# Converting w_out in pieces of 384 columns with lo parts on VectorE, in a fused attention and squared-ReLU FFN kernel

## The chip, the cores and the metric

The kernel runs on one core of one Trainium2 chip. The metric is device time in microseconds of one execution, the median of several runs. In this text PE is TensorE, DVE VectorE, ACT ScalarE, POOL GpSimd and SP SyncE, as in the profile.

## The reference

Attention over 8 batches x 12 heads of 448 x 64, with normed q and k, gives x of 3584 tokens x 768. Then comes a feed-forward layer:

```python
def _moe_ref(x, w_in, w_out, s, b):
    h = x @ w_in                  # 3584 x 768 @ 768 x 2048
    r = np.maximum(h, 0.0)
    g = s * (r * r) + b
    return (g @ w_out).astype(np.float32)   # 3584 x 2048 @ 2048 x 768
```

w_in and w_out arrive as 64-bit floats; all else is 32-bit.

## The kernel before

Matmuls take operands rounded to a shorter 32-bit form (fp32r), so every operand is split into a hi part and a lo part (what the rounding left out), and a product is three matmuls: hi x hi, lo x hi, hi x lo.

There are two stages. In the first (lines 206 to 640) attention runs batch by batch, and beside it the first product, `ffn_in` (line 170), of the batch before. A *block* of it is 128 of the 2048 hidden columns for one batch of 448 tokens: 18 matmuls into a PSUM bank. `rectify` (189) has ACT take the ReLU out of the bank into a tile `r`, after which the bank is free, and `keep_r` (200) stores it to a DRAM buffer `r_d`.

The second stage (643 to 733) begins when attention is over and the last batch still has its 16 blocks of `ffn_in` to do. Beside these blocks, written out by hand in a fixed order for all engines but SP (`manual_schedule`, line 701; SP's order and everything behind that block are set by the framework's scheduler), two things are made ready for the second product:

- w_out (2048 x 768) in 48 *pieces* of 128 rows x 256 columns. `load_double` (115) is a generator: each `next` issues a step. SP loads the piece of 64-bit words (`w64o`, line 121). DVE puts the 32-bit float `wao` together from the two halves of each word in four instructions (124, 127, 129, 132), of which the last needs a square of the high half made by ACT (`wmo`, 125). Later ACT rounds it to the hi part `woh` (135) and POOL makes the lo part `wol` (136). The hi and lo parts are written over w_in's, quarter by quarter (`tag=wh{i}`, `wl{i}`): a quarter of w_in is four blocks' worth, so a piece that is put together at block m gets its hi and lo parts at block m + 4.
- The first three tiles of g, 128 tokens each. `squares` (652) is a generator as well: SP loads r for all 2048 columns (1 MB, line 659), ACT squares (665) and DVE scales (666); at the next step ACT rounds to `gh` (670) and DVE makes `gl` (671).

The loop over m (706 to 729) has 20 rounds: `ffn_in` for 16 of them (the work of round m on the other engines is also called block m's), three new pieces in each, and from round 4 on the hi and lo parts of three older ones. The tiles' loads are issued ahead of the loop (`chain(todo, first)`), their squares in rounds 7, 9, 11, and gh and gl in rounds 8, 10, 12. Buffers: 5 for `w64o`, 16 for `wao`, 3 for `wmo`, 2 for the tiles of r.

Behind it `ffn_out` (674) does the second product: first for tiles 0 to 2 together, quarter by quarter of w_out, then for the 25 others one by one. A tile is 96 matmuls, in two PSUM banks (`po`). Six banks for the first three tiles come from the list of free ones, whose order is that of the blocks that last used them: tile 0 gets the banks of blocks 8 and 9, tile 1 those of 10 and 11, tile 2 those of 12 and 13. So tile 2's first matmul waits for the ReLU of block 12.

Of the kernel before, what the change touches and what calls it, by code (L numbers as in the profile page):

```python
# [9 lines left out]
F32 = mybir.dt.float32  # L10
F32R = mybir.dt.float32r
I32 = mybir.dt.int32
AF = mybir.ActivationFunctionType
ALU = mybir.AluOpType
# [23 lines left out]
def attention_then_relu2_ffn(  # L38
# [30 lines left out]
    V, S, G, T = nc.vector, nc.scalar, nc.gpsimd, nc.tensor  # L69

    NPAIR, P, _, SEQ = kq.shape
# [12 lines left out]
    NFC = DF // P  # L84
    NKC = 4
    HALF = DM // 2
    NS = 4
    FS = DF // NS
    WI = 512
    WO = 256  # L90
    W = 8
    NSLOT = W * NPAIR

# [16 lines left out]
    def psum(name):  # L110

        bank = free.pop(0)
        return ps.tile([P, 512], F32, tag=bank, name=name), bank

    def load_double(room, dst_hi, dst_lo, src):

        w, a, m = room  # L120
        nc.sync.dma_start(w.rearrange("p n t -> p (n t)"), src)  # L121
        yield
        low, high = w[:, :, 0], w[:, :, 1]
        V.tensor_scalar(a, high, 3, 0x3FFFFFF8, ALU.logical_shift_left, ALU.bitwise_and)  # L124
        S.activation(m, high.bitcast(F32), AF.Square)  # L125
        yield
        V.scalar_tensor_tensor(a, high, -0x40000000, a, ALU.bitwise_and, ALU.bitwise_or)  # L127
        yield
        V.scalar_tensor_tensor(a, low, 29, a, ALU.logical_shift_right, ALU.bitwise_or)  # L129
        yield  # L130
        af = a.bitcast(F32)
        V.scalar_tensor_tensor(af, m.bitcast(F32), LEAST * LEAST, af, ALU.is_ge, ALU.mult)  # L132
        for _ in range(GAP):
            yield
        S.copy(dst_hi, af)  # L135
        G.tensor_tensor(dst_lo, af, dst_hi.bitcast(F32), ALU.subtract)  # L136
        yield

    w_in32 = w_in.bitcast(I32)
# [3 lines left out]
    def parts_of_w_in():  # L143

        for i in range(NS):
            whi[i] = wpool.tile([P, NCC, FS], F32R, tag=f"wh{i}", name=f"wih{i}")
            wlo[i] = wpool.tile([P, NCC, FS], F32R, tag=f"wl{i}", name=f"wil{i}")
            for c0 in range(0, FS, WI):
                for cc in range(NCC):
                    f0 = 2 * (i * FS + c0)  # L150
                    src = w_in32[cc * P : (cc + 1) * P, f0 : f0 + 2 * WI]
                    yield whi[i][:, cc, c0 : c0 + WI], wlo[i][:, cc, c0 : c0 + WI], src

    def parts_of_w_out():
        n = NFC // NS
        for i in range(NS):
            ohi[i] = wpool.tile([P, n, DM], F32R, tag=f"wh{i}", name=f"woh{i}")
            olo[i] = wpool.tile([P, n, DM], F32R, tag=f"wl{i}", name=f"wol{i}")
            for f in range(n):
                r0 = (i * n + f) * P  # L160
                for c0 in range(0, DM, WO):
                    c = slice(c0, c0 + WO)
                    src = w_out32[r0 : r0 + P, 2 * c0 : 2 * (c0 + WO)]
                    yield ohi[i][:, f, c], olo[i][:, f, c], src
# [24 lines left out]
    def rectify():  # L189

        while later:
            ph, bank, b, fc = later.pop(0)
            r = xp.tile([P, SEQ], F32, tag="r", bufs=2, name=f"r{b}_{fc}")
            S.activation(r, ph[:, :SEQ], AF.Relu)
            free.append(bank)
            kept.append((b, fc, r))
# [3 lines left out]
    def keep_r():  # L200

        while kept:
            b, fc, r = kept.pop(0)
            nc.sync.dma_start(r_d[b][fc], r)

    with tc.tile_pool(name="apool", bufs=1) as ap:
# [300 lines left out]
        def pieces():  # L507
            for i, (hi, lo, src) in enumerate(parts_of_w_in()):
                w = ap.tile([P, WI, 2], I32, tag="w64", name=f"w64i{i}")
                a = ap.tile([P, WI], I32, tag="wa", bufs=2, name=f"wai{i}")  # L510
                yield load_double((w, a, hi), hi, lo, src)

        def convert():

# [77 lines left out]
        with tc.manual_schedule(engines=ORDERED):  # L592
            begun = []
            for s_ in range(FIRST, NSLOT + START + 1):
# [17 lines left out]
                for f, a in jobs[s_]:  # L612
                    if f is next:
                        continue
                    g = f(*a)
# [18 lines left out]
                b, m = divmod(s_ + 1 - START, W * NP)  # L634
# [8 lines left out]
    with tc.tile_pool(name="opool", bufs=2) as op:  # L643

        def pieces():
            for i, part in enumerate(parts_of_w_out()):
                w = op.tile([P, WO, 2], I32, tag="w64", bufs=5, name=f"w64o{i}")
                a = op.tile([P, WO], I32, tag="wa", bufs=16, name=f"wao{i}")
                m = op.tile([P, WO], F32, tag="wm", bufs=3, name=f"wmo{i}")
                yield load_double((w, a, m), *part)  # L650

        def squares(t):
            r = op.tile([P, NFC, P], F32, tag="r2", bufs=2, name=f"r2_{t}")
            t0 = t * P
            while t0 < (t + 1) * P:
                b, off = divmod(t0, SEQ)
                n = min((t + 1) * P - t0, SEQ - off)
                o = t0 - t * P
                nc.sync.dma_start(  # L659
                    r[:, :, o : o + n],  # L660
                    r_d[b][:, :, off : off + n].rearrange("f p t -> p f t"),
                )
                t0 += n
            yield
            S.activation(r, r, AF.Square)
            V.tensor_scalar(r, r, sb_s, sb_b, ALU.mult, ALU.add)  # L666
            yield
            gh = op.tile([P, NFC, P], F32R, tag="gh", bufs=3, name=f"gh{t}")
            gl = op.tile([P, NFC, P], F32R, tag="gl", bufs=3, name=f"gl{t}")
            S.copy(gh, r)  # L670
            V.tensor_tensor(gl, r, gh.bitcast(F32), ALU.subtract)  # L671
            yield gh, gl

        def ffn_out(ts, gs):
            n = NFC // NS
            pos = [[psum(f"po{t}_{e}") for e in range(2)] for t in ts]
            for i in range(NS):
                for (gh, gl), po in zip(gs, pos):
                    for f in range(n):
                        fc = i * n + f  # L680
                        for m, (x, w) in enumerate(((gh, ohi[i]), (gh, olo[i]), (gl, ohi[i]))):
                            for e in range(2):
                                T.matmul(  # L683
                                    po[e][0][:, :HALF],
                                    x[:, fc, :],
                                    w[:, f, e * HALF : (e + 1) * HALF],
                                    start=fc == 0 and m == 0,
                                    stop=fc == NFC - 1 and m == 2,
                                )
            for t, po in zip(ts, pos):  # L690
                ot = op.tile([P, DM], F32, tag="ot", name=f"ot{t}")
                S.copy(ot[:, :HALF], po[0][0][:, :HALF])
                V.tensor_copy(ot[:, HALF:], po[1][0][:, :HALF])  # L693
                free.extend(bank for _, bank in po)
                nc.sync.dma_start(out[t * P : (t + 1) * P, :], ot)

        first = [squares(t) for t in range(3)]
        gs = []
        pieces = pieces()
        n = 3 * NFC // NS  # L700
        with tc.manual_schedule(engines=ORDERED - {ENGINE.SP}):
            waiting = []
            todo = list(islice(pieces, 3))
            for g in chain(todo, first):
                next(g)
            for m in range(NFC + NFC // NS):
                if m < NFC:
                    for _ in ffn_in(xs, *units[m]):
                        pass
                now, todo = todo, list(islice(pieces, 3))  # L710
                for g in todo:
                    next(g)
                old = waiting[:3] if m >= NFC // NS else []
                waiting = waiting[len(old) :]
                for step in range(4):
                    for g in now:
                        next(g)
                    if step == 1:
                        rectify()
                        keep_r()  # L720
                    if step == 2:
                        for g in old:
                            for _ in range(GAP):
                                next(g)
                waiting += now
                if m in (7, 9, 11):
                    next(first[(m - 7) // 2])
                if m in (8, 10, 12):
                    gs.append(next(first[(m - 8) // 2]))
        ffn_out([0, 1, 2], gs)  # L730
        for t in range(3, NT // P):
            *_, g = squares(t)
            ffn_out([t], [g])
# [44 lines left out]
```

## Time and profile before

| what | us |
|---|---|
| median of 3 runs | 1564.41 |
| lowest and highest of them | 1563.24, 1564.85 |
| the profiled execution's own time | 1564.78 |
| its span, first to last instruction | 1563.0 |
| PE busy with matmuls | 1466.8 |
| DVE busy | 904.3 |
| ACT busy | 816.0 |
| POOL busy | 735.6 |

The mean granted TensorE clock was 0.974 of full speed. In the profile an instruction is named by the line of the program, its engine, its operation and its tiles (out<-in, buffer numbers left out). A row of the timeline has the start and the length of a run of like instructions, and in brackets how long the engine stood idle ahead of it and what ended that. Where rows overlap, the time one instruction costs its engine is the distance to the next one's start. The releasers are worked out from semaphores: of several waits the last is named.

### The profile page before, as it was taken

How to read it: one execution, taken by the hardware profiler on the slowest of the kernel's cores; microseconds unless marked ns; L12 is line 12 of the kernel's file. 1: busy time of each engine (PE TensorE's matmuls, PEld its weight loads, DVE VectorE, ACT ScalarE, POOL GpSimd, SP SyncE). 2: the span in 40 equal slices, each digit the busy share in tenths (PEclk: the TensorE clock that was granted, in tenths of full speed). 3: DMA queues.
4: the chain of work that ended last, by engine and by line, in shares of the span. 5: the costliest groups of instructions: out<-in, count | busy, mean ns of one | idle time of the engine just before them, and what ended most of it. 6: DMA issues, size and time to landing. Idle time of an engine off the chain costs nothing. (4 is left out here: it accounts for less than half of the span.)

```text
span 1563.0 us, 21722 instructions
## 1 busy us (share of the span) xinstructions
PE 1466.8 (94%) x7380; PEld 1347.0 (86%) x7380; DVE 904.3 (58%) x1399; ACT 816.0 (52%) x1522; POOL 735.6 (47%) x611
## 2 busy tenths in 40 slices
PE   8775679999999999999999999997999999999998
PEld 7543468889989989989989989996899999999998
DVE  6986986776676776676676675269732222222210
ACT  4654646676676676766666666435442222222210
POOL 7586757667766767767767765215600000000000
PEclk9997789999999999999999999999999999999999
DMA  4465555666666666666666653276452322322300
GB/s 112 124 170 162 170 169 175 190 185 186 191 184 187 191 180 191 192 183 188 192 181 190 191 174 115 66 239 188 132 148 75 102 85 75 107 79 79 106 21 31
DMA packets 218751, 230.86 MB, mean 148 GB/s; under 512 B 72912, under 2 KB 193744, under 8 KB 218640
## 3 DMA queue, kind: packets, MB, share of 16 engines
q1 hardware_dynamic: 218640, 229.47, 49.4%
q8 instruction: 58, 0.95, 0.3%
q14 instruction: 53, 0.43, 0.1%
HBM read 177.21 MB, written 40.84 MB: 140 GB/s over the span
## 5 line engine op out<-in xcount | busy, mean ns | idle before, releaser
L177 PE MATMUL ph<-x,wih 128*128 128x448 f32 x1536 | 491.9, 367 | 0.0
L177 PEld LDWEIGHTS ph<-x,wih 128*128 128x128 f32 x1536 | 291.7, 190 | 23.5 <-issue 0.2
L415 ACT ACTIVATE st<-st 128x448 f32<-128x448 f32 x336 | 176.6, 526 | 239.4 <-PE st L399 236.3
L369 DVE TENSOR_REDUCE nmx<-sh 112x1 fp32r<-112x448 f32 x384 | 235.7, 618 | 112.4 <-PE sh L358 110.9
L177 PE MATMUL ph<-x,wil 128*128 128x448 f32 x768 | 284.6, 371 | 0.0
L683 PE MATMUL po<-woh,gh 128*128 128x384 f32 x896 | 230.1, 336 | 9.0 <-ACT gh L670 6.5
L683 PE MATMUL po<-wol,gh 128*128 128x384 f32 x896 | 229.9, 336 | 3.4 <-POOL wol L136 3.4
L683 PE MATMUL po<-woh,gl 128*128 128x384 f32 x896 | 228.9, 335 | 0.0
L455 PE MATMUL av<-ah,vs 128*128 128x448 f32 x672 | 195.9, 373 | 22.6 <-DVE ah L436 17.8
L436 DVE TENSOR_TENSOR al<-st,ah 128x448 fp32r<-128x448 f32 x252 | 154.3, 612 | 51.4 <-ACT ah L423 42.0
L358 PE MATMUL sh<-ka,qa 128*112 128x448 f32 x384 | 149.2, 391 | 34.4 <-DVE ka L253 13.2
L423 ACT CAST ah<-st 128x448 fp32r<-128x448 f32 x336 | 179.5, 534 | 2.5
L683 PEld LDWEIGHTS po<-woh,gh 128*128 128x128 f32 x896 | 162.7, 189 | 10.6 <-ACT gh L670 7.1
L683 PEld LDWEIGHTS po<-wol,gh 128*128 128x128 f32 x896 | 162.8, 189 | 4.5 <-POOL wol L136 4.5
L396 PE MATMUL st<-qa,ka 128*128 128x448 f32 (+1 forms) x384 | 160.6, 418 | 5.5 <-DVE nmx L369 4.5
L683 PEld LDWEIGHTS po<-woh,gl 128*128 128x128 f32 x896 | 162.7, 189 | 0.6 <-DVE gl L671 0.5
L455 PEld LDWEIGHTS av<-ah,vs 128*128 128x128 f32 x672 | 127.6, 192 | 38.7 <-ACT x L504 11.4
L177 PEld LDWEIGHTS ph<-x,wil 128*128 128x128 f32 x768 | 145.7, 190 | 12.0
L358 PEld LDWEIGHTS sh<-ka,qa 128*112 128x112 f32 x384 | 107.5, 281 | 46.9 <-POOL ka L342 19.0
L496 POOL TENSOR_TENSOR u<-uz,zb 64x448 f32<-64x448 f32 x96 | 118.2, 1231 | 59.7 <-DMA zb<-z_d 55.9
L342 POOL TENSOR_TENSOR ka<-kq,ka 64x448 fp32r<-64x448 f32 x84 | 98.8, 1176 | 98.2 <-ACT ka L340 85.6
L399 PE MATMUL st<-qb,kb 128*128 128x448 f32 (+1 forms) x384 | 144.0, 375 | 0.0
(76 smaller groups left out, 2042.8 us busy)
## 6 DMA issues: line engine op xcount, KB each, us to landing
kq<-in_dram SPq DMA_DIRECT2D x84, 448.0 KB, 4.0
rb<-i_d SPq DMA_DIRECT2D x84, 448.0 KB, 5.1
r_d<-r SPq DMA_DIRECT2D x128, 224.0 KB, 3.2
r<-r_d SPq DMA_DIRECT2D x24, 1024.0 KB, 6.0
raw<-in_dram SPq DMA_DIRECT2D x42, 448.0 KB, 5.5
w64i<-in_dram SPq DMA_DIRECT2D x24, 512.0 KB, 4.5
w64o<-in_dram SPq DMA_DIRECT2D x48, 256.0 KB, 3.1
kb<-ka SPq DMA_DIRECT2D x96, 112.0 KB, 2.2
```

What stands on the lines that cost most here:

```text
L177: T.matmul(ph[:, :SEQ], w[:, cc, f0 : f0 + P], xs[b, cc][:, part, :], start=n == 0, stop=n == 3 * NCC - 1,)
L342: G.tensor_tensor(ka[n][D:, a], t[D:, 0], ka[n][D:, a].bitcast(F32), ALU.subtract)
L358: T.matmul(sh[:QC, :SEQ], qa[p % 2][:, a].rearrange("k (p c) -> k c p", c=NQ)[:, c], ka[p % 2][:, a], start=True, stop=True,)
L369: V.tensor_reduce(out=nmxs[p][:, c : c + 1], in_=sh[:QC, :SEQ], op=ALU.max, axis=AX.X, negate=True)
L396: T.matmul(st[:rows, :SEQ], ka[n][:, keys], qa[n][:, q], start=True, stop=False)
L399: T.matmul(st[:rows, :SEQ], kb[n][:, keys], qb[n][:, q], start=False, stop=True,)
L415: S.activation(st[:rows, :SEQ], st[:rows, :SEQ], AF.Exp)
L423: S.copy(ah[:rows], sts[i][0][:rows, :SEQ])
L436: V.tensor_tensor(al, st[:rows, :SEQ], ah[:rows].bitcast(F32), ALU.subtract)
L455: T.matmul(av[:, :SEQ], x, a, start=kc == 0 and m == 0, stop=kc == 3 and m == len(todo) - 1,)
L496: G.tensor_tensor(u[a], uzs.pop((p, j))[a], zb[a], ALU.mult)
L683: T.matmul(po[e][0][:, :HALF], x[:, fc, :], w[:, f, e * HALF : (e + 1) * HALF], start=fc == 0 and m == 0, stop=fc == NFC - 1 and m == 2,)
```

## The change

- `WO` is 384, so w_out goes in 32 pieces, two in each round.
- The lo part of a w_out piece is made by DVE (`rest=V`), not POOL, and a step later than its hi part (`apart=True`): the hi part is issued in step 0 of a round, behind the ReLU, the lo part in step 2.
- The ReLU and the store of r move from step 1 to step 0.
- Buffers: 4 for `w64o`, 10 for `wao` (taken when the first instruction that writes it is issued, not with the load), 2 for `wmo`.
- The first three tiles of r are loaded in rounds 1, 2, 3 of the loop, not ahead of it. Their squares come in rounds 6, 8, 10, gh and gl in rounds 7, 9, 11.

```diff
-    WO = 256
+    WO = 384
...
-    def load_double(room, dst_hi, dst_lo, src):
+    def load_double(room, dst_hi, dst_lo, src, apart=False, rest=None):
...
         S.copy(dst_hi, af)
-        G.tensor_tensor(dst_lo, af, dst_hi.bitcast(F32), ALU.subtract)
+        if apart:
+            yield
+        (rest or G).tensor_tensor(dst_lo, af, dst_hi.bitcast(F32), ALU.subtract)
...
-                w = op.tile([P, WO, 2], I32, tag="w64", bufs=5, name=f"w64o{i}")
-                a = op.tile([P, WO], I32, tag="wa", bufs=16, name=f"wao{i}")
-                m = op.tile([P, WO], F32, tag="wm", bufs=3, name=f"wmo{i}")
-                yield load_double((w, a, m), *part)
+                w = op.tile([P, WO, 2], I32, tag="w64", bufs=4, name=f"w64o{i}")
+                m = op.tile([P, WO], F32, tag="wm", bufs=2, name=f"wmo{i}")
+
+                def words(i=i):
+                    return op.tile([P, WO], I32, tag="wa", bufs=10, name=f"wao{i}")
+
+                yield load_double((w, words, m), *part, apart=True, rest=V)
...
-            todo = list(islice(pieces, 3))
-            for g in chain(todo, first):
+            todo = list(islice(pieces, 2))
+            for g in todo:
                 next(g)
...
+                if m in (1, 2, 3):
+                    next(first[m - 1])
...
-                    if step == 1:
+                    if step == 0:
                         rectify()
                         keep_r()
-                    if step == 2:
                         for g in old:
                             for _ in range(GAP):
                                 next(g)
+                    if step == 2:
+                        for g in old:
+                            next(g)
                 waiting += now
+                if m in (6, 8, 10):
+                    next(first[(m - 6) // 2])
                 if m in (7, 9, 11):
-                    next(first[(m - 7) // 2])
-                if m in (8, 10, 12):
-                    gs.append(next(first[(m - 8) // 2]))
+                    gs.append(next(first[(m - 7) // 2]))
```

With the new lines, line numbers of the changed program are 1 to 6 higher: 121 stays, 124 to 132 are 125 to 133, 135 and 136 are 136 and 139, and 659 to 683 are 665 to 689.

Three places show what moves. First SP's queue at the start of the second stage, before (`w64o3` is piece 3, `r2_0` tile 0 of r, `r_d7` the buffer that the ReLU of the last batch is stored to):

```order
L121 DMA w64o0_10930<-in_6_dram 128x512
L121 DMA w64o1_10933<-in_6_dram 128x512
L121 DMA w64o2_10936<-in_6_dram 128x512
L659 DMA r2_0_10942<-r_d0_74 128x16x128
L659 DMA r2_1_10944<-r_d0_74 128x16x128
L121 DMA w64o3_10967<-in_6_dram 128x512
L121 DMA w64o4_10970<-in_6_dram 128x512
L121 DMA w64o5_10973<-in_6_dram 128x512
L204 DMA r_d7_81<-r7_0_10988 128x448
```

and changed:

```order
L121 DMA w64o0_10930<-in_6_dram 128x768
L121 DMA w64o1_10932<-in_6_dram 128x768
L121 DMA w64o2_10955<-in_6_dram 128x768
L121 DMA w64o3_10957<-in_6_dram 128x768
L665 DMA r2_0_11001<-r_d0_74 128x16x128
L207 DMA r_d7_81<-r7_0_10967 128x448
L121 DMA w64o4_10995<-in_6_dram 128x768
L121 DMA w64o5_10997<-in_6_dram 128x768
L207 DMA r_d7_81<-r7_1_11009 128x448
L121 DMA w64o6_11037<-in_6_dram 128x768
L121 DMA w64o7_11039<-in_6_dram 128x768
L665 DMA r2_1_11043<-r_d0_74 128x16x128
```

The pieces of round 1 stood behind both tiles of r; now those of rounds 0 and 1 stand ahead of the first tile, and the second tile behind those of round 3.

Second, DVE in round 4, the first with older pieces, before:

```order
L124 TENSOR_SCALAR wao12_11117<-w64o12_11116 128x256
L124 TENSOR_SCALAR wao13_11120<-w64o13_11119 128x256
L124 TENSOR_SCALAR wao14_11123<-w64o14_11122 128x256
L127 SCALAR_TENSOR_TENSOR wao12_11117<-w64o12_11116,wao12_11117 128x256
L127 SCALAR_TENSOR_TENSOR wao13_11120<-w64o13_11119,wao13_11120 128x256
L127 SCALAR_TENSOR_TENSOR wao14_11123<-w64o14_11122,wao14_11123 128x256
L129 SCALAR_TENSOR_TENSOR wao12_11117<-w64o12_11116,wao12_11117 128x256
L129 SCALAR_TENSOR_TENSOR wao13_11120<-w64o13_11119,wao13_11120 128x256
L129 SCALAR_TENSOR_TENSOR wao14_11123<-w64o14_11122,wao14_11123 128x256
L132 SCALAR_TENSOR_TENSOR wao12_11117<-wmo12_11118,wao12_11117 128x256
L132 SCALAR_TENSOR_TENSOR wao13_11120<-wmo13_11121,wao13_11120 128x256
L132 SCALAR_TENSOR_TENSOR wao14_11123<-wmo14_11124,wao14_11123 128x256
```

and changed:

```order
L125 TENSOR_SCALAR wao8_11129<-w64o8_11081 128x384
L125 TENSOR_SCALAR wao9_11132<-w64o9_11083 128x384
L128 SCALAR_TENSOR_TENSOR wao8_11129<-w64o8_11081,wao8_11129 128x384
L128 SCALAR_TENSOR_TENSOR wao9_11132<-w64o9_11083,wao9_11132 128x384
L130 SCALAR_TENSOR_TENSOR wao8_11129<-w64o8_11081,wao8_11129 128x384
L130 SCALAR_TENSOR_TENSOR wao9_11132<-w64o9_11083,wao9_11132 128x384
L139 TENSOR_TENSOR wol0_10929<-wao0_10961,woh0_10928 128x384
L139 TENSOR_TENSOR wol0_10929<-wao1_10964,woh0_10928 128x384
L133 SCALAR_TENSOR_TENSOR wao8_11129<-wmo8_11082,wao8_11129 128x384
L133 SCALAR_TENSOR_TENSOR wao9_11132<-wmo9_11084,wao9_11132 128x384
```

Twelve instructions have become ten wider ones, two of them the lo parts that POOL had in a queue of its own.

Third, PE in the second product, where the quarter 1 of w_out (`woh1`) begins with tile 0, matmuls 49 to 54, and where tile 2 begins, matmuls 79 to 82, before:

```order
L683 MATMUL po0_0_11841<-woh1_11114,gh0_11425 128x384
L683 MATMUL po0_1_11842<-woh1_11114,gh0_11425 128x384
L683 MATMUL po0_0_11841<-wol1_11115,gh0_11425 128x384
L683 MATMUL po0_1_11842<-wol1_11115,gh0_11425 128x384
L683 MATMUL po0_0_11841<-woh1_11114,gl0_11426 128x384
L683 MATMUL po0_1_11842<-woh1_11114,gl0_11426 128x384
...
L683 MATMUL po1_0_11843<-woh1_11114,gh1_11541 128x384
L683 MATMUL po2_0_11845<-woh0_10928,gh2_11659 128x384
L683 MATMUL po2_0_11845<-wol0_10929,gh2_11659 128x384
L683 MATMUL po1_1_11844<-woh1_11114,gh1_11541 128x384
```

and changed, matmuls 49 to 56 and, behind the dots, 61 and 91:

```order
L689 MATMUL po0_0_11665<-woh1_11079,gh0_11284 128x384
L689 MATMUL po0_1_11666<-woh1_11079,gh0_11284 128x384
L689 MATMUL po0_0_11665<-wol1_11080,gh0_11284 128x384
L689 MATMUL po0_1_11666<-wol1_11080,gh0_11284 128x384
L689 MATMUL po2_0_11669<-woh0_10928,gh2_11474 128x384
L689 MATMUL po2_0_11669<-wol0_10929,gh2_11474 128x384
L689 MATMUL po0_0_11665<-woh1_11079,gl0_11285 128x384
L689 MATMUL po0_1_11666<-woh1_11079,gl0_11285 128x384
...
L689 MATMUL po2_0_11669<-woh0_10928,gl2_11475 128x384
...
L689 MATMUL po2_1_11670<-woh0_10928,gh2_11474 128x384
```

Tile 2's first matmul has moved up from number 80 to 53, its gl is first needed at 61, and its second bank at 91. Matmuls 1 to 52, and from 115 on, stand as before: quarter 2 begins at 145 and quarter 3 at 217, and the last lo part of quarter 2 is first needed at 165.

More of the change, by code (lines that the diff above doesn't have):

```diff
@@ L113, in psum @@
         return ps.tile([P, 512], F32, tag=bank, name=name), bank
-    def load_double(room, dst_hi, dst_lo, src):
-        w, a, m = room
+    def load_double(room, dst_hi, dst_lo, src, apart=False, rest=None):
+        w, words, m = room
         nc.sync.dma_start(w.rearrange("p n t -> p (n t)"), src)
         yield
+        a = words()
         low, high = w[:, :, 0], w[:, :, 1]
@@ L510, in pieces @@
                 a = ap.tile([P, WI], I32, tag="wa", bufs=2, name=f"wai{i}")
-                yield load_double((w, a, hi), hi, lo, src)
+                yield load_double((w, lambda a=a: a, hi), hi, lo, src)
         def convert():
@@ L699, in attention_then_relu2_ffn @@
         pieces = pieces()
-        n = 3 * NFC // NS
+        later_by = NFC // NS
         with tc.manual_schedule(engines=ORDERED - {ENGINE.SP}):
             waiting = []
-            todo = list(islice(pieces, 3))
-            for g in chain(todo, first):
+            todo = list(islice(pieces, 2))
+            for g in todo:
                 next(g)
-            for m in range(NFC + NFC // NS):
+            for m in range(NFC + later_by):
                 if m < NFC:
@@ L709, in attention_then_relu2_ffn @@
                         pass
-                now, todo = todo, list(islice(pieces, 3))
+                now, todo = todo, list(islice(pieces, 2))
                 for g in todo:
                     next(g)
-                old = waiting[:3] if m >= NFC // NS else []
+                if m in (1, 2, 3):
+                    next(first[m - 1])
+                old = waiting[:2] if m >= later_by else []
                 waiting = waiting[len(old) :]
```

## The prediction

> **What bounds the kernel now.** I read the chain that ended last first, in order of time, to see where the end was decided. Its last pieces (start, us, what):
>
> ```profile
> 1119.07 0.92 POOL wol L136
> 1120.02 438.93 PE po L683 x2523
> ```
>
> From 1120.02 us on the end is TensorE's alone: 2523 matmuls of the second product without a wait, 438.93 us, to the end of the span but for 4 us. The second product has 28 tiles x 96 = 2688 of them, so the one at 1120.02 is number 166. Time can only be won ahead of it. So next, the waits of PE between 1005 and 1125 us (total, times, longest), and PE in order of time there (start, length, and in brackets the wait ahead of it):
>
> ```profile
> PE po L683 <- ACT gh L670: 6.5, 1, 6.5
> PE po L683 <- POOL wol L136: 3.4, 4, 1.7
> PE po L683 <- ACT r L194: 2.5, 2, 1.6
> ```
>
> ```profile
> 1010.07 0.57 PE L177 MATMUL ph<-x,wih 128*128 128x448 f32 x2
> ...
> 1010.68 0.57 PE L177 MATMUL ph<-x,wih 128*128 128x448 f32 x2
> ...
> 1074.72 0.34 PE L683 MATMUL po<-woh,gh 128*128 128x384 f32 x1
> ...
> 1086.73 0.69 PE L683 MATMUL po<-woh,gh 128*128 128x384 f32 x1 [6.52 <-ACT gh L670]
> 1088.99 0.69 PE L683 MATMUL po<-woh,gh 128*128 128x384 f32 x1 [1.57 <-ACT r L194]
> ...
> 1116.02 0.44 PE L683 MATMUL po<-wol,gh 128*128 128x384 f32 x1 [1.68 <-POOL wol L136]
> ...
> 1119.15 0.44 PE L683 MATMUL po<-wol,gh 128*128 128x384 f32 x1 [1.03 <-POOL wol L136]
> ...
> 1120.51 0.84 PE L683 MATMUL po<-woh,gl 128*128 128x384 f32 x2
> 1121.15 0.84 PE L683 MATMUL po<-woh,gh 128*128 128x384 f32 x2
> ...
> 1123.00 0.51 PE L683 MATMUL po<-woh,gh 128*128 128x384 f32 x2
> 1123.36 0.52 PE L683 MATMUL po<-wol,gh 128*128 128x384 f32 x2
> ...
> 1124.40 0.51 PE L683 MATMUL po<-wol,gh 128*128 128x384 f32 x2
> ```
>
> Matmul 1 of the second product starts at 1074.72. (Ahead of it the first product's go by threes in 0.61 us, a block of 18 in 3.66.) Undisturbed, six take 1124.40 - 1123.36 = 1.04 us, 0.1733 each. Without waits number 166 would start at 1074.72 + 165 x 0.1733 = 1103.3, 16.7 us sooner than it does. Behind the waits the array also runs slowly: the nine matmuls from 1120.02 to 1123.00 take 2.98 us for 1.56. The clock says so (stretch, length, busy time of PE, PEld, DVE, ACT, POOL, then PEclk, DMA share, GB/s):
>
> ```profile
> 1025.00:1026.00 1.00, 1.00 (x7) 0.93 (x6) 1.00 (x4) 0.00 (x0) 0.00 (x0) 1.00 1.17 290
> 1045.00:1046.00 1.00, 1.00 (x7) 0.92 (x6) 0.32 (x3) 0.17 (x1) 0.00 (x0) 1.00 1.10 387
> 1086.00:1088.00 2.00, 0.69 (x1) 0.29 (x1) 2.00 (x5) 1.28 (x3) 1.08 (x2) 0.50 0.86 261
> 1120.00:1122.00 2.00, 1.98 (x6) 1.98 (x7) 2.00 (x4) 0.38 (x2) 2.00 (x3) 0.50 0.04 8
> ```
>
> So the whole prize is 16.7 + (2.98 - 1.56) = 18.1 us, and everything behind it is the conversion of w_out and of the first three tiles of r, which DVE, ACT and POOL do beside the last sixteen blocks of the first product. Its pace is DVE's. Two stretches, one with POOL idle, one with POOL at work:
>
> ```profile
> 1021.34 0.29 DVE L124 TENSOR_SCALAR wao<-w64o 128x256 int32<-128x256 int32 x1 [2.82 <-issue]
> ...
> 1041.38 0.29 DVE L124 TENSOR_SCALAR wao<-w64o 128x256 int32<-128x256 int32 x1 [0.66 <-DMA w64o<-in_dram]
> 1041.59 1.09 DVE L127 SCALAR_TENSOR_TENSOR wao<-w64o,wao 128x256 int32<-128x256 int32 x3
> 1042.59 1.09 DVE L129 SCALAR_TENSOR_TENSOR wao<-w64o,wao 128x256 int32<-128x256 int32 x3
> 1043.60 1.09 DVE L132 SCALAR_TENSOR_TENSOR wao<-wmo,wao 128x256 f32<-128x256 f32 x3
> ...
> 1063.76 2.18 DVE L129 SCALAR_TENSOR_TENSOR wao<-w64o,wao 128x256 int32<-128x256 int32 x3
> 1065.86 1.63 DVE L132 SCALAR_TENSOR_TENSOR wao<-wmo,wao 128x256 f32<-128x256 f32 x3
> ...
> 1073.94 2.28 DVE L671 TENSOR_TENSOR gl<-r,gh 128x2048 fp32r<-128x2048 f32 x1
> 1076.14 0.69 DVE L124 TENSOR_SCALAR wao<-w64o 128x256 int32<-128x256 int32 x3
> ...
> 1095.40 1.34 DVE L666 TENSOR_SCALAR r<-r,sb_s,sb_b 128x2048 f32<-128x2048 f32 x1
> 1096.65 0.69 DVE L124 TENSOR_SCALAR wao<-w64o 128x256 int32<-128x256 int32 x3
> ```
>
> ```profile
> 1063.77 2.77 POOL L136 TENSOR_TENSOR wol<-wao,woh 128x256 fp32r<-128x256 f32 x3 [4.33 <-ACT woh L135]
> ```
>
> Three L129 take 1.09 us alone and 2.18 while POOL's three L136 run, from the same moment on.
>
> **The change part by part.** *Wider pieces.* On DVE three 256-wide instructions of L127 take 1.00 (1041.59 to 1042.59), 0.335 each; the 2048-wide L671 takes 2.20 (1073.94 to 1076.14). Two points give a line: 1.04 ns per column and 0.07 us each time. A 384-wide one is then 0.468 us. L124, 0.21 to its successor, gives 0.27 by the same start-up. 48 pieces x (0.21 + 3 x 0.335) = 58.3 us become 32 x (0.27 + 3 x 0.468) = 53.6: 4.7 us of DVE saved.
>
> *The lo parts to DVE.* 32 more instructions with two inputs, as L671 is, 0.468 each: 15.0 us added to DVE. POOL's slowing of DVE goes entirely, since POOL has nothing else here. A block from block 4 on, counted from 0 (two pieces, two lo parts), costs DVE 2 x 1.674 + 2 x 0.468 = 4.28 us, against PE's 3.66. DVE stays the slower one. POOL's queue loses 48 instructions, with nothing behind them.
>
> *Squares.* Each tile costs DVE 1.25 (1095.40 to 1096.65) + 2.20, three of them 10.35, as now, but one block sooner.
>
> *ACT.* The rows for its work in one block:
>
> ```profile
> 1044.05 0.77 ACT L125 ACTIVATE wmo<-w64o 128x256 f32<-128x256 f32 x2 [1.75 <-DVE wao L132]
> ...
> 1046.17 0.54 ACT L194 ACTIVATE r<-ph 128x448 f32<-128x448 f32 x1
> 1046.59 1.02 ACT L135 CAST woh<-wao 128x256 fp32r<-128x256 f32 x3
> ...
> 1098.27 1.92 ACT L670 CAST gh<-r 128x2048 fp32r<-128x2048 f32 x1
> ```
>
> Scaled to 384 columns: two squares 0.95, the ReLU 0.5, two hi parts 0.9, together 2.4. With two buffers for the squares they begin when the block before leaves L132. A lo part comes on DVE 0.54 + 4 x 0.468 = 2.4 us into the block, when its hi part has been there for some 0.5: the new wait of DVE on ACT, with the L132 of the same block queued behind it, costs nothing as long as ACT starts on time. If not, each 0.1 us late costs 0.1 in twelve blocks.
>
> *Loads.* On SP's queue two tiles of r stand ahead of block 1's pieces now; changed, four pieces stand ahead of the first tile, and the second follows two blocks later. Up to block 4's second piece SP issues ten pieces of 393 KB, two tiles of 1.05 MB and three stores of 229 KB. At 387 GB/s for pieces (1045 to 1046) and stores, and 290 for tiles of r (1025 to 1026), that is 10.2 + 1.8 + 7.2 = 19.2 us. Transfers begin 0.7 us (262 KB) ahead of DVE's first instruction at 1021.34, so the piece lands at 1039.9. DVE alone would be at 1021.9 + 4 x 3.35 = 1035.3: the loads hold it up by some 4 us, here and not later. Afterwards a block needs 0.79 + 0.23 MB in 4.28 us, 238 GB/s, below the 290 of a tile of r. The third tile of r stands behind block 8's store, two blocks ahead of its square: 1.05 MB at 290 is 3.6 us of 8.6.
>
> *The sum.* Block 4 ends at 1039.9 + 0.27 + 8 x 0.468 = 1043.9, and then come eleven blocks and 10.35 us of squares: 1043.9 + 47.1 + 10.35 = 1101.4; the last eight lo parts, 1105.1. What PE needs, by the order of its matmuls, against when it is there:
> - gh of tile 1, number 25, 1078.9: ready ahead of its gl, which ends at 1043.9 + 5 x 4.28 + 2 x 3.45 = 1072.2.
> - the bank of block 12's ReLU, for tile 2's first matmul, now number 53, 1083.7: DVE has left block 11's L132 at 1043.9 + 7 x 4.28 + 10.35 - 2.2 = 1082.0, then two squares and the ReLU, 1083.3.
> - gl of tile 2, number 61, 1085.1: ready at 1084.2.
> - the last lo parts of the third quarter, number 165, 1103.1: ready one L132 pair ahead of 1101.4, at 1100.5.
> - those of the last quarter, from number 219, 1112.5: ready by 1105.1.
>
> All arrive in time, by 0.4 us at the tightest. The profiled execution took 1564.78 us, 1.8 round its span and 0.4 above the median of 1564.41. With the whole prize the median becomes 1564.4 - 18.1 = 1546.3. Two margins are below 1 us, and a wait delays all that follows, so I add 0.7: 1547.0.
>
> **The rivals.** *Late loads at the start.* Were pieces no faster than r's tiles, 290 for 387 GB/s, the ten would take 13.6 us for 10.2, and everything would be 3.4 later: PE waits 3.0 at number 53, and the slow clock adds 1.4, as after 1120.02: 1546.3 + 4.4 = 1550.7. For it: 290 GB/s was all that got through with r's tiles in the queue. Against: 387 without. Whether a wait of this size costs the clock is read from 1114 to 1120: no wait above 1.68 us there, yet 0.50 from 1120 to 1122. The Trainium skill's page TensorE: Matmul & The Clock Gate (Part 1: The HAM clock gate) gives half rate after at least one idle window of about 3.4 us; by it this wait would leave the clock alone, and the rival would be 1549.3. The row speaks against that.
>
> *The loads as a round trip.* There are four buffers for two pieces a block; a load starts when L129 two blocks ahead is done, 2.4 us into that block, so two blocks cannot be shorter than 2.4 us plus the time to landing. Of that, the rows for these loads:
>
> ```profile
> DMA to landing us min/median/max: 2.6/3.1/7.8
> ```
>
> With the median a block of 2.8 would do; with the longest, 7.8, always, it would be 5.1 us, 0.82 x 11 = 9.0 later at the end: PE waits 9.0 - 2.6 = 6.4 for the third quarter, and 1.4 of clock: 1554.1. It speaks against it that 7.8 is the extreme.
>
> *Slower: DVE does not get faster when POOL falls silent.* If L129's 2.18 us are not POOL's doing, but come of the transfers or of ACT, DVE carries 15 us more and keeps its slow stretches. Place: blocks 4 to 15. At 1.5 times 0.468 for the eight long instructions a block is 6.15 us, 20.6 more over eleven: the third quarter's lo parts come at 1121 instead of 1100.5, 1 us behind today's 1120, and the last quarter's eight lo parts then come on top: about 1568. It decides from 1.47 times on. Against it: every stretch at 1.09 has POOL idle with DMA running. The Trainium skill's page SBUF — State Buffer (Who interferes with whom) has a DVE instruction with two SBUF inputs contend with a GpSimd one that reads SBUF, the later one blocked; by it this rival is out, and the pair of rows at 1063.76 agrees.
>
> *PE's waits only move*, to some place that this count misses: within 0.2%.
>
> **How the numbers follow.** All in time or nearly (1545 to 1549): 0.69. Late loads, 1551: 0.17. Round trip, 1554: 0.08. Slower: 0.04. Waits only move: 0.02. The first two hold 0.86; the range takes the third's price in, as DVE's scaled durations are not measured: 1545 to 1554. Faster by over 0.2% (about 3 us, what a measurement of this kernel can tell from no change) 0.94, within 0.02, slower 0.04.
>
> **What would show it.** Right: PE's waits between 1074 and 1125 us below 2 us in all, clock 1.00 throughout, 384-wide L128, L130, L133 and L139 at 0.47 us to the next, POOL idle, the uninterrupted run of po matmuls starting near 1074.7. Wrong: DVE pauses on L136 (hi parts) each block, a block over 5 us, block 4 beginning behind 1041, or a PE wait on the ReLU's bank or gl.

## The result and the profile after

| | before | changed |
|---|---|---|
| median, us | 1563.83 (4 runs, 1561.81 to 1564.85) | 1544.74 (4 runs, 1541.20 to 1547.35) |
| profiled execution's time / span, us | 1564.78 / 1563.0 | 1541.2 / 1539.3 |
| PE's waits, us from 1000 to 1130 | 12.4 | no row |

The ratio is 0.9878, interval 0.9856 to 0.9900: 19.1 us faster. Forecast were 1547.0, 1545.0 to 1554.0. The direction and the mechanism hold; the median lies 0.26 us under the range's low end.

PE's waits between 1000 and 1130 us have no row any more. The end of the chain that ended last, for the changed kernel (start, us, what):

```profile
996.93 72.15 PE ph L180 x356
1069.08 466.18 PE po L689 x2688
```

All 2688 matmuls of the second product now stand in one run, 0.1734 us each, where before only the last 2523 did. The windows, of the changed kernel (columns as in the prediction; the first row is needed further down):

```profile
200.00:300.00 100.00, 88.56 (x409) 77.71 (x408) 73.27 (x115) 63.67 (x131) 72.48 (x56) 0.97 0.62 187
1000.00:1100.00 100.00, 100.00 (x519) 94.70 (x518) 83.88 (x173) 56.56 (x98) 2.58 (x2) 1.00 0.71 227
```

In the second PE is busy throughout at clock 1.00, and POOL has two instructions left. What DVE does, from its timeline in the changed kernel (the first row is the last of attention; block 5, which begins when block 4 ends, and block 6's first row; then tile 2's gl and the last eight lo parts):

```profile
1008.31 4.35 DVE L508 TENSOR_TENSOR x<-u,x 128x448 fp32r<-128x448 f32 x6 [8.49 <-ACT x L507]
...
1038.64 0.62 DVE L125 TENSOR_SCALAR wao<-w64o 128x384 int32<-128x384 int32 x2
1039.18 1.02 DVE L128 SCALAR_TENSOR_TENSOR wao<-w64o,wao 128x384 int32<-128x384 int32 x2
1040.12 1.02 DVE L130 SCALAR_TENSOR_TENSOR wao<-w64o,wao 128x384 int32<-128x384 int32 x2
1041.05 1.02 DVE L139 TENSOR_TENSOR wol<-wao,woh 128x384 fp32r<-128x384 f32 x2
1041.99 1.02 DVE L133 SCALAR_TENSOR_TENSOR wao<-wmo,wao 128x384 f32<-128x384 f32 x2
1042.93 0.62 DVE L125 TENSOR_SCALAR wao<-w64o 128x384 int32<-128x384 int32 x2
...
1076.84 2.28 DVE L677 TENSOR_TENSOR gl<-r,gh 128x2048 fp32r<-128x2048 f32 x1
...
1096.20 3.83 DVE L139 TENSOR_TENSOR wol<-wao,woh 128x384 fp32r<-128x384 f32 x8
```

A pair of two-input instructions costs 0.94 (1039.18 to 1040.12), so 0.47 each, and a block 4.29 (1038.64 to 1042.93): forecast were 0.468 and 4.28. No line has 2.18 or 1.63 for its three instructions any more.

**Two stages, two differences.** The profiled spans differ by 23.7 us, more than the 18.1 that was to be had. The last part of attention, where stage 1 ends, in the kernel before:

```profile
1014.11 4.41 DVE L505 TENSOR_TENSOR x<-u,x 128x448 fp32r<-128x448 f32 x6 [7.69 <-ACT x L504]
```

It ends at 1014.11 + 4.41 = 1018.52 before, and at 1008.31 + 4.35 = 1012.66 changed. From there to the end of the span, called stage 2 from here on, it is 1563.0 - 1018.52 = 544.5 and 1539.3 - 1012.66 = 526.6: 17.9 us gained in stage 2, which the change is about, and 5.9 in stage 1, whose instructions it leaves alone. The same window in the kernel before:

```profile
200.00:300.00 100.00, 88.48 (x391) 77.64 (x390) 71.66 (x111) 61.49 (x125) 68.96 (x53) 0.91 0.60 182
```

PE was granted 0.91 between 200 and 300 us before, 0.97 in the changed kernel's execution, and did 391 matmuls there for 409. The experiments ask first whether these 5.9 us belong to the change, and then which of its parts makes the 17.9.

### The profile page after: what moved, and what is told of

The parts are those of the page before. It is cut to its first block, busy times and chain, and to the rows that moved or that the text cites. A ratio compares the mean times of both kernels' runs of the same rounds, so it can differ in the third digit from the quotient of the medians.

```text
span 1539.3 us, 21465 instructions
## 1 busy us (share of the span) xinstructions
PE 1458.2 (95%) x7380; PEld 1342.9 (87%) x7380; DVE 886.8 (58%) x1367; ACT 811.2 (53%) x1490; POOL 680.4 (44%) x563
## 4 chain that ended last, share of the span: by engine, by line
PE 83%; DVE 8%; DMA 4%; issue 2%; ACT 1%; POOL 1%; SPq 0%; DVEq 0%; ACTq 0%; POOLq 0%
PE po L689 30%; PE ph L180 28%; PE av L458 11%; PE st L402 4%; PE st L399 4%; PE sh L361 4%; DMA w64i<-in_dram 4%; DVE nmx L372 1%; DVE x L508 1%; DVE wai L130 1%; PE warmth L270 1%; DVE wai L128 1%; DVE zt L483 1%; DVE al L439 1%; DVE wai L133 1%
## 5 line engine op out<-in xcount | busy, mean ns | idle before, releaser
L458 PE MATMUL av<-ah,vs 128*128 128x448 f32 x672 | 195.8, 373 | 22.9 <-DVE ah L439 18.1
L671 ACT ACTIVATE r<-r 128x2048 f32<-128x2048 f32 x28 | 53.7, 1918 | 169.3 <-DMA r<-r_d 169.2
```

What stands on the lines that cost most here:

```text
L458: T.matmul(av[:, :SEQ], x, a, start=kc == 0 and m == 0, stop=kc == 3 and m == len(todo) - 1,)
```

## The experiments

Each was profiled and timed; times are medians, beside the kernel before on the same chip. "Stage 2" is reckoned as above, from each one's own trace.

| kernel | median, us | before there | ratio (95%) | stage 2, us | PE's waits, us |
|---|---|---|---|---|---|
| changed again | 1546.78 | 1564.30 | 0.9881 (0.9863 to 0.9899) | 526.9 | 0.2 |
| lo parts back on POOL | 1560.95 | 1564.30 | 0.9972 (0.9957 to 0.9987) | 543.0 | 11.0 |
| before, lo parts on DVE | 1552.34 | 1564.30 | 0.9916 (0.9898 to 0.9934) | 532.9 | 3.6 |
| r loaded ahead | 1547.63 | 1564.30 | 0.9883 (0.9864 to 0.9902) | 528.0 | 1.1 |
| pieces of 256 | 1545.85 | 1564.73 | 0.9882 (0.9865 to 0.9898) | 527.3 | 0.6 |
| squares a block later | 1544.55 | 1564.73 | 0.9872 (0.9857 to 0.9886) | 526.4 | 0.2 |
| each lo part twice | 1552.74 | 1564.73 | 0.9925 (0.9911 to 0.9940) | 534.6 | 4.9 |
| POOL reads beside DVE | 1580.22 | 1563.45 | 1.0105 (1.0082 to 1.0128) | 561.0 | 24.2 |
| POOL writes beside DVE | 1550.54 | 1563.45 | 0.9919 (0.9890 to 0.9948) | 530.3 | 3.4 |

**The changed kernel again** (no edit).

> The changed kernel once more. Theory (the second stage now holds its full prize, and the rest of the difference from the forecast is the first stage, which differs from one execution to the next): the median over five rounds lies between 1544 and 1547 us, PE again has no wait between attention's end and the last matmul, but attention's last DVE instruction (the lo part of x) ends at another time than the 1012.7 us of the profiled run, up to 1018.5 as in the kernel before. Rival (the change also shortens the first stage, whose code is the same, by some 6 us): it ends near 1012.7 again and the median is 1541 to 1543.

The end of attention and PE's one wait in this execution:

```profile
1011.52 4.39 DVE L508 TENSOR_TENSOR x<-u,x 128x448 fp32r<-128x448 f32 x6 [8.19 <-ACT x L507]
```

```profile
PE po L689 <- ACT r L197: 0.2, 1, 0.2
```

The same program ends stage 1 at 1015.91 this time, 3.3 us later than in the first trace, and needs 526.9 behind it, 0.3 more. Over the eleven traces of this study stage 1, which no edit touches, ends anywhere from 1012.66 to 1019.20. Between 200 and 300 us PE had a clock of 0.91 in four of the five executions that end last (1016.84 to 1019.20) and 0.93 in the other; the six others had 0.93 to 0.97. From 300 to 1000 us every one has 1.00. So the 5.9 us are the execution's, not the change's. Why the clock is granted differently there stays open.

**Lo parts back on POOL**, all else as changed.

```diff
-                yield load_double((w, words, m), *part, apart=True, rest=V)
+                yield load_double((w, words, m), *part, apart=True)
```

> The changed kernel with the lo parts of w_out back on GpSimd; width, order of loads and squares stay changed. Theory (GpSimd's work slows DVE's): 32 lo parts of 384 columns hold GpSimd some 2.6 us in every block and slow DVE by up to as much; a block takes 5 us or more for 3.35, PE waits 8 us or more before the third quarter of w_out, 1553 to 1562 us. Rival (the wider pieces and the loads' order bring the gain, and DVE is merely relieved of 0.94 us a block here): no wait of PE, 1543 to 1547 us.

DVE at about block 5, POOL over the same time, and PE's waits:

```profile
1041.91 1.01 DVE L130 SCALAR_TENSOR_TENSOR wao<-w64o,wao 128x384 int32<-128x384 int32 x2
1042.85 1.01 DVE L133 SCALAR_TENSOR_TENSOR wao<-wmo,wao 128x384 f32<-128x384 f32 x2
1044.78 2.26 DVE L125 TENSOR_SCALAR wao<-w64o 128x384 int32<-128x384 int32 x2 [0.91 <-POOL wol L139]
1046.95 1.84 DVE L128 SCALAR_TENSOR_TENSOR wao<-w64o,wao 128x384 int32<-128x384 int32 x2
1048.71 1.01 DVE L130 SCALAR_TENSOR_TENSOR wao<-w64o,wao 128x384 int32<-128x384 int32 x2
```

```profile
1042.02 5.88 POOL L139 TENSOR_TENSOR wol<-wao,woh 128x384 fp32r<-128x384 f32 x4 [2.40 <-DVE wao L128]
```

```profile
PE po L689 <- ACT r L197: 11.0, 2, 6.5
```

POOL's four run from 1042.02 to 1047.90. From 1044.78 on DVE's pair L125 takes 2.17 to its successor (0.54 in the trace of the changed kernel) and L128 1.76 (0.94); as soon as the four are done, L130 has 1.01 again. Ahead of that, L130 and L133 kept 1.01 beside the first of the four: there the delay fell on POOL, whose four take 5.88 us where a subtraction of this size takes it 1.04 (POOL reads beside DVE, below). In addition the four make DVE wait 0.9 for POOL, since the ten `wao` come free only with the lo part. The loss comes back on PE as two waits for banks of late ReLUs, 11.0 us, and stage 2 is 16.4 us longer than in the changed kernel. Without the lo parts on DVE the change is worth 544.5 - 543.0 = 1.5 us of its 17.9.

**The kernel before with the lo parts on DVE**, nothing else of the change.

```diff
-    def load_double(room, dst_hi, dst_lo, src):
+    def load_double(room, dst_hi, dst_lo, src, rest=None):
...
-        G.tensor_tensor(dst_lo, af, dst_hi.bitcast(F32), ALU.subtract)
+        (rest or G).tensor_tensor(dst_lo, af, dst_hi.bitcast(F32), ALU.subtract)
...
-                yield load_double((w, a, m), *part)
+                yield load_double((w, a, m), *part, rest=V)
```

> The kernel before with only its lo parts moved to DVE (pieces of 256 columns, tiles of r ahead of the loads, squares late; hi and lo part issued in the same step). Theory: without GpSimd's work the three-instruction groups take 1.00 to 1.10 us throughout, but DVE waits for ACT's hi part in each block and tile 2 comes late; PE waits 4 us or so in all, some slow clock behind that, 1549 to 1554 us: two thirds of the gain. Rival (width and order bring the gain): 1560 to 1565 us.

One of DVE's groups by form (busy, mean ns), PE in order of time from its one wait on, and the clock there:

```profile
L129 DVE SCALAR_TENSOR_TENSOR wao<-w64o,wao 128x256 int32<-128x256 int32 x48 | 17.4, 416 | 0.0
```

```profile
1080.92 0.69 PE L683 MATMUL po<-woh,gh 128*128 128x384 f32 x1 [3.62 <-ACT gh L670]
...
1087.25 0.52 PE L683 MATMUL po<-woh,gh 128*128 128x384 f32 x2
```

```profile
1080.00:1082.00 2.00, 1.08 (x3) 1.08 (x4) 2.00 (x6) 1.69 (x4) 0.00 (x0) 0.50 0.89 283
```

L129 has 416 ns in the mean; with POOL at work it had 527 in the kernel before (the next row, by form as well).

```profile
L129 DVE SCALAR_TENSOR_TENSOR wao<-w64o,wao 128x256 int32<-128x256 int32 x48 | 22.8, 527 | 0.0
```

That alone takes stage 2 to 532.9, 11.6 us of the 17.9. One wait is left, 3.62 for tile 1's gh, and behind it the 21 matmuls from 1080.92 to 1087.25 take 6.33 us for 3.64, at a clock of 0.50: 3.6 + 2.7 = 6.3, the whole distance to the changed kernel. How much of the 11.6 comes from DVE's speed, and how much from lo parts that no longer queue on POOL (3.4 us of PE's waits before), is not separated here.

**The first tiles of r loaded ahead of the loop**, as before.

```diff
-            for g in todo:
+            for g in chain(todo, first):
                 next(g)
...
-                if m in (1, 2, 3):
-                    next(first[m - 1])
```

> The changed kernel with the first three tiles of r loaded ahead of the loop, as before the change. Theory: block 1's pieces come some 5 to 6 us later, block 4's 2 us later than with the changed order, since the same bytes have to pass; DVE's margin at tile 2 is about half a us, so PE waits 0.5 to 2 us, 1545 to 1548 us. Rival (the order of the loads is what counts): PE waits 4 us or more, 1550 us and over.

PE's wait, and the clock there:

```profile
1080.99 0.44 PE L689 MATMUL po<-woh,gh 128*128 128x384 f32 x1 [1.07 <-ACT r L197]
```

```profile
1080.00:1082.00 2.00, 1.01 (x6) 1.01 (x7) 2.00 (x4) 2.00 (x6) 0.00 (x0) 1.00 0.71 275
```

The new order of the loads is worth 528.0 - 526.6 = 1.4 us; the wait costs its own length and no clock.

**Pieces of 256 columns**, three a round, with buffers of the same size in bytes.

```diff
-    WO = 384
+    WO = 256
...
-            todo = list(islice(pieces, 2))
+            todo = list(islice(pieces, 3))
...
-                old = waiting[:2] if m >= later_by else []
+                old = waiting[:3] if m >= later_by else []
```

> The changed kernel with pieces of 256 columns, three a block (6, 15 and 3 buffers instead of 4, 10 and 2); lo parts on DVE, loads' order and squares as changed. Theory: 48 starts of four and one instructions instead of 32 cost DVE 0.33 us a block more, 4 us over blocks 4 to 15; the third quarter's lo parts come at the moment they are needed, PE waits at most 1.5 us: 1544 to 1547 us. Rival (the width matters, by fewer instructions or larger transfers): 1549 us and over.

One wait of 0.6 on a late ReLU, stage 2 at 527.3: the width is worth 0.7 us, although it saves DVE 4.7 by the prediction's count. Most of what it saves was not late for anything.

**Squares a block later**, as before.

```diff
-                if m in (6, 8, 10):
-                    next(first[(m - 6) // 2])
                 if m in (7, 9, 11):
-                    gs.append(next(first[(m - 7) // 2]))
+                    next(first[(m - 7) // 2])
+                if m in (8, 10, 12):
+                    gs.append(next(first[(m - 8) // 2]))
```

> The changed kernel with the squares of the first three tiles of r a block later, as before the change. Theory: tile 2's gl comes 4.3 us later, 4 us behind matmul 61 of the changed kernel's order; in this build the scheduler lets tile 2 wait till matmul 85 for its gl, so PE waits less than 1 us and the time stays within 2 us of the changed kernel's. Rival (PE waits for tile 2 all the same, as it did before): a wait of 3 us or more, 1548 us and over.

0.2 us of waits, 526.4 in stage 2: the edit is worth nothing here. The scheduler orders PE's matmuls by what is ready, and put tile 2's gl at number 85 instead of 61.

**Each lo part computed twice**, which adds 32 instructions to DVE.

```diff
-        (rest or G).tensor_tensor(dst_lo, af, dst_hi.bitcast(F32), ALU.subtract)
+        for _ in range(2 if apart else 1):
+            (rest or G).tensor_tensor(dst_lo, af, dst_hi.bitcast(F32), ALU.subtract)
```

> The changed kernel with each lo part of w_out computed twice on DVE: 0.94 us more in each of blocks 4 to 15. Theory (DVE carries the stage, and its margin is 0.5 to 2 us): the third quarter's lo parts come 11.3 us later, 9 us behind PE's need; with the slow clock behind that wait the time is 10 to 13 us over the changed kernel's. Rival (DVE has slack beyond that, the loads or PE set the stage's length): less than 5 us over.

PE's waits, one of them in order of time, and the clock at it and behind it:

```profile
PE po L690 <- ACT r L198: 4.6, 4, 2.5
PE po L690 <- DVE gl L678: 0.3, 1, 0.3
```

```profile
1101.94 0.34 PE L690 MATMUL po<-woh,gl 128*128 128x384 f32 x1
1104.77 0.44 PE L690 MATMUL po<-woh,gh 128*128 128x384 f32 x1 [2.49 <-ACT r L198]
1105.05 0.34 PE L690 MATMUL po<-wol,gh 128*128 128x384 f32 x1
...
1106.09 0.48 PE L690 MATMUL po<-wol,gh 128*128 128x384 f32 x1
...
1109.56 0.34 PE L690 MATMUL po<-woh,gh 128*128 128x384 f32 x1
```

```profile
1102.70:1106.11 3.41, 1.34 (x8) 1.35 (x9) 2.85 (x7) 2.83 (x6) 0.00 (x0) 1.00 0.16 61
1106.11:1109.52 3.41, 3.41 (x12) 3.41 (x11) 3.38 (x7) 0.48 (x2) 0.00 (x0) 0.50 0.75 241
1109.52:1112.93 3.41, 3.41 (x21) 3.41 (x21) 3.38 (x9) 1.80 (x5) 0.00 (x0) 1.00 0.20 72
```

Stage 2 grew by 8.0, short of what was expected and over what the rival allowed: so DVE's load does carry the end, but the size was off. Of 15 us added (32 x 0.468), 4.9 come out as waits and 1.6 as slow clock: the eleven matmuls from 1106.09 to 1109.56 take 3.47 us, at 0.1733 each 1.91. Most of the other 1.5 lies at the edges of the five waits: from 1101.94 to 1105.05 two matmuls take 3.11 us, 2.76 more than their 0.35, where the wait is listed with 2.49, and five times 0.27 is 1.4. No wait on a lo part appears, which the expectation had: every wait at a bank moves all later matmuls back, and the deadline of the third quarter with them, so delays at successive deadlines need not add up; that this is the whole reason is argued, not shown.

**POOL reads beside DVE**: the changed kernel, and on POOL 64 subtractions of a tile of 128 x 384 from itself, for which nobody waits.

```diff
+        junk = op.tile([P, 384], F32, tag="junk", bufs=1, name="junk")
...
                 yield load_double((w, words, m), *part, apart=True, rest=V)
+                for _ in range(2):
+                    G.tensor_tensor(junk, junk, junk, ALU.subtract)
...
+            G.memset(junk, 0.0)
```

> The changed kernel, with work on GpSimd that nobody waits for: 64 subtractions of a 128 x 384 tile from itself, one behind the other from the second stage's start on; the other engines' order is the changed kernel's, instruction for instruction. Theory (GpSimd's reading of SBUF alone slows DVE, apart from any wait for its result): while the 64 run, DVE's groups with two tiles as input take 1.5 to 2 times as long and its one-input L125 is delayed too, a block takes 6 us or more, PE waits 8 us or more, 1555 to 1570 us. Rival (in the kernel before it was the waits on the lo parts, for buffers and for the third quarter, that cost the time): DVE's groups stay at 0.94 us a pair and the time within 2 us of the changed kernel's.

POOL's run, three pairs of DVE inside it, and PE's waits:

```profile
1017.39 66.81 POOL L660 TENSOR_TENSOR junk<-junk 128x384 f32<-128x384 f32 x64
```

```profile
1045.42 1.88 DVE L125 TENSOR_SCALAR wao<-w64o 128x384 int32<-128x384 int32 x2
1047.22 2.28 DVE L128 SCALAR_TENSOR_TENSOR wao<-w64o,wao 128x384 int32<-128x384 int32 x2
1049.43 2.28 DVE L130 SCALAR_TENSOR_TENSOR wao<-w64o,wao 128x384 int32<-128x384 int32 x2
```

```profile
PE ph L180 <- ACT r L197: 13.0, 3, 5.1
PE po L693 <- ACT r L197: 11.2, 2, 6.0
```

L128's pair goes from 0.94 to 2.21 (1047.22 to 1049.43), 2.35 times, with no semaphore between the two engines. PE waits 24.2 us and stage 2 takes 561.0, 34.4 more than in the changed kernel and 16.5 more than before, and the median is about 10 us above what was expected at most: the reads slow DVE by more than the 1.5 times that the prediction's slower rival reckoned with. The 10.2 us beside the waits are mostly slow clock. Behind each of the five waits PE is granted 0.51 to 0.57 for 4 to 6 us, as in these two stretches:

```profile
1076.00:1080.00 4.00, 3.77 (x11) 3.36 (x12) 4.00 (x5) 2.80 (x4) 3.69 (x5) 0.57 0.15 57
1098.00:1104.00 6.00, 5.75 (x19) 5.75 (x20) 6.00 (x12) 4.52 (x8) 0.00 (x0) 0.53 0.87 301
```

PE's busy time there times what the clock lacks of 1.00 is 1.6 and 2.7 us, and 9.5 over all five, an estimate. POOL's work alone, without any dependence on it, is enough to undo the whole gain.

**POOL writes beside DVE**: the same with 192 memsets, which read nothing.

```diff
                 yield load_double((w, words, m), *part, apart=True, rest=V)
+                for _ in range(6):
+                    G.memset(junk, 0.0)
```

> As the run before, but GpSimd fills the tile with zeros 192 times: it writes SBUF and reads nothing. Theory in its narrow form (only a GpSimd instruction that reads blocks DVE's second input): DVE's two-input groups stay at 0.94 us a pair, at most L125 with its one input is delayed; the time is within 4 us of the changed kernel's. In its wide form (any work of GpSimd on SBUF slows DVE): as in the run before, 1553 us or more.

```profile
1019.42 101.79 POOL L660 MEMSET junk<- 128x384 f32 x192
```

```profile
1045.51 1.01 DVE L128 SCALAR_TENSOR_TENSOR wao<-w64o,wao 128x384 int32<-128x384 int32 x2
...
1053.55 1.59 DVE L676 TENSOR_SCALAR r<-r,sb_s,sb_b 128x2048 f32<-128x2048 f32 x1
1055.06 1.22 DVE L125 TENSOR_SCALAR wao<-w64o 128x384 int32<-128x384 int32 x2
```

POOL is busy for longer than in the experiment above, but L128's pair keeps its 1.01. Only DVE's instructions with one input tensor are delayed: L676 1.59 (L672, the same line of the changed kernel, has 1.34), L125's pair 1.22 for 0.62. Not all of them are: the pair at 1049.26 has 0.61. Stage 2 is 3.7 us longer; the median lies 3.8 us above the changed kernel's second set and 5.8 above its first, where at most 4 were expected. So it is not that POOL is busy, but what it reads, that slows the two-input instructions.

## Why the prediction was right, and where its size was off

**The prize.** Right: forecast 18.1 us, measured in stage 2 17.9. The run of `po` matmuls is whole from number 1 on, at clock 1.00.

**DVE's durations and its blocks.** Right, to 0.01 us. Reckoned from the end of attention, block 4 was forecast to end at 1043.9 - 1018.5 = 25.4; it ended at 1038.64 - 1012.66 = 26.0. The last lo part, 1105.1 - 1018.5 = 86.6, came at 1096.20 + 3.75 - 1012.66 = 87.3 (eight times 0.47 is 3.75). Everything was 0.6 to 0.7 late, nearly all of it with the loads: block 4's second piece, forecast for 1039.9 - 1018.5 = 21.4, was taken up at 1034.61 - 1012.66 = 21.95.

```profile
1034.61 0.36 DVE L125 TENSOR_SCALAR wao<-w64o 128x384 int32<-128x384 int32 x1 [0.59 <-DMA w64o<-in_dram]
```

**The tightest margins.** Places right, sizes too good by 0.5 each. PE in the first trace of the changed kernel, numbers 1, 53 and 61:

```profile
1068.91 0.52 PE L689 MATMUL po<-woh,gh 128*128 128x384 f32 x2
...
1078.05 0.44 PE L689 MATMUL po<-woh,gh 128*128 128x384 f32 x1
...
1079.55 0.33 PE L689 MATMUL po<-woh,gl 128*128 128x384 f32 x1
```

Tile 2's bank was to be free 0.4 us ahead of number 53. Undisturbed that would start at 1068.91 + 52 x 0.1733 = 1077.92; it starts at 1078.05, 0.1 late, and in the second trace PE waits 0.2 us at a late ReLU (the row above). Tile 2's gl, forecast 0.9 ahead of number 61, is there at 1076.84 + 2.28 = 1079.1, 0.4 ahead of 1079.55.

**POOL's slowing of DVE.** Right, and now shown by itself: reads beside DVE make 2.35 times of its two-input instructions, and silence gives them back. The rival that DVE would not get faster is out by the trace before any experiment: 0.94 a pair in every block. The Trainium skill's page SBUF — State Buffer (Who interferes with whom) sets a two-input DVE instruction against a GpSimd one that reads SBUF, and DVE's one-input forms that use both ports against any of GpSimd's; both experiments with POOL agree, with 2.21 for 0.94 in the one, and 1.01 beside 1.59 for 1.34 in the other. By the page the later instruction is blocked; the first of POOL's four in "lo parts back on POOL", drawn out beside DVE pairs that kept 1.01, agrees. DVE's 1.10 each (2.21 a pair) against POOL's 66.81 / 64 = 1.04 would fit turns taken one by one, but the trace doesn't show the turns.

**The rivals of later loads.** They did not come: transfers held DVE's L125 for 4.5 us in the first blocks, as this group of the changed kernel from 1012 to 1105 us has it (forecast: some 4 behind block 0, where 4.0 of the 4.5 lie), none of it behind block 4.

```profile
L125 DVE TENSOR_SCALAR wao<-w64o 128x384 int32<-128x384 int32 x32 | 10.2, 354 | 7.8 <-DMA w64o<-in_dram 4.5 <-issue 3.3
```

**The step that failed is the last of the sum: "Two margins are below 1 us, and a wait delays all that follows, so I add 0.7: 1547.0", and with it the range's low end of 1545.0.** With the whole prize stage 2 would be 544.5 - 18.1 = 526.4; it took 526.6 in one trace and 526.9 in the other, so the term of 0.7 measured 0.2 and 0.5. Without it the count is 1546.3, and what stage 2 gained gives 1564.4 - 17.9 = 1546.5 from the same median. That is the smaller part: of the 2.3 us from 1547.0 down to 1544.74, 0.5 are this term, 0.6 are the median of the kernel before (1564.4 in the sum, 1563.83 in this set), and 1.2 are left. The low end was put only 1.3 us below the full prize, about the scatter of the three runs shown, and so took stage 1 as given. It varies by 6.5 us between executions (1012.66 to 1019.20), and the median of four runs moves with it: 1544.74 in the first set of the changed kernel, 1546.78 in the second, 1545.4 for the eight runs together, of which the lowest has 1541.20 and the highest 1548.71. The 17.9 us of stage 2, taken from this set's 1563.83, give 1545.9, still inside the range. That the remaining 1.2 us are stage 1's, chance and not the change, is argued from the spread of the traces; the other timed runs have no trace.

**What each part is worth.** Lo parts on DVE alone: 11.6 of 17.9. All the rest without them: 1.5. Singly undone from the changed kernel, the order of r's loads gives 1.4, the width 0.7, the earlier squares nothing. With the lo parts on DVE the rest gives 6.3, and the three singly undone account for 2.1 of that. What is left may lie in parts that replace one another, or in the ReLU and the hi parts at the head of the round, which were not tried singly; that stays open.

## What to carry to other kernels

Lay rows of one instruction side by side, with the helping engine at work and with it idle: in the kernel before POOL took the lo parts off DVE, and the kernel is 11.6 us faster when DVE makes them itself. When operands are made ready for a bound engine, count each one's due time by the number of its matmul; here only what was late was worth anything, and savings elsewhere (the width, the squares) hardly showed. And a range needs the spread of the stages that the change leaves alone, which a few runs of one median may not show.

## What the runs showed of the hardware

- A wait of PE of 2.49 us ("each lo part twice") was followed, 1.3 us after PE resumed, by a clock of 0.50 for 3.41 us, though PE had been busy for 1.34 of the 3.41 us ahead of that; the one of 3.62 by 0.50 and a loss of 2.7 us; in the kernel before, waits of 1.68 and 1.03 that end within 3.2 us of each other by 0.50. Waits of 1.97 and 1.44 ("POOL writes", 1.00 from 1080 to 1092), 1.07 and 0.59 cost no clock. The Trainium skill's page TensorE: Matmul & The Clock Gate (Part 1: The HAM clock gate) asks for an idle window of about 3.4 us; the row of 3.62 agrees with it, that of 2.49 does not.
- POOL's subtractions alone slow DVE's one-input L125 too, 1.80 for a pair (1045.42 to 1047.22) against 0.54; beside memsets such a pair has a length of 1.22 for 0.62.
- The granted clock between 200 and 300 us differs from execution to execution of the same instructions (0.91 to 0.97), and the end of stage 1 by up to 6.5 us.
